# FFN inputs turned on TensorE instead of by DMA, h written as z(1+y), and block 0's butterflies on TensorE, in a long-convolution plus SwiGLU kernel

## The chip, the cores and the metric

The kernel runs on one core of a Trainium2 chip. The metric is the device time of one execution in microseconds (us). The kernel before takes 307.82 us, the median of three runs.

In this text PE is TensorE, DVE is VectorE, ACT is ScalarE, POOL is GpSimd and SP is SyncE, which here only issues DMAs.

## What is computed

A sequence of 2048 rows of 640 features goes through two stages. With `LN` a layer normalization without gain or bias:

```python
def _A_ref(q, k, v, shift_k, ssm_k, ssm_D):     # q is LN(A_q)
    k_shift = sum(k_pad[:, t:t+S, :] * shift_k[:, 3-t] for t in range(4))
    kv = k_shift * v
    y = irfft(rfft(kv_pad) * rfft(ssm_k_pad))[:, :S]    # causal convolution over the sequence
    return q * (y + kv * ssm_D)
h  = A_q + _A_ref(LN(A_q), A_k, A_v, ...)
h2 = h + (silu(LN(h) @ w_gate) * (LN(h) @ w_up)) @ w_down
```

S is 2048, the FFN has 1728 hidden features, and inputs and output are bf16.

## The kernel before

**Tiling.** The sequence is cut into four blocks of 512 rows. The convolution is a product of block transforms: each block of kv is transformed by cosine and sine matmuls (`x_transform`, L725), each block of the filter likewise (`g_transform`, L670), the products are summed over pairs of blocks on DVE (L939, L975, L979, L999, L1000), and `back` brings block i into the time domain (L810). A transformed block is two "lanes" of 128 x 3 x 1280 numbers; the third part is the sum of the first two and serves the three-multiplication complex product. Lanes that are needed later go to DRAM and come back.

**Forward transform.** For each block it makes sums over the even and over the odd rows separately (eight PSUM tiles of 128 x 640 with four matmuls each, L725). ACT or DVE evacuates them. Then four DVE operations, the butterflies, form sum (L735) and difference (L738), and two more form the third part (L742).

**From convolution to h.** `ln_stats` takes mean and mean square of each row group of x with two ACT passes (L750, L752), a few tiny DVE operations and one power on POOL (L764). `back` writes z = x - mean (L796). y comes out of PSUM scaled by 1/sigma (L397). DVE multiplies z by y (L816) and adds x (L817); this is h. `ln_stats` then runs on h, for the first pair of row groups (r = 0) and for the second (r = 1).

**FFN input.** Two DVE passes for each r write hn = LN(h) (L824). Each of a block's four row groups of 128 x 640 is then turned by one DMA transpose on SP's queue (`tr_dma`, L595) into `hlnT`, the right-hand side of the FFN's first matmuls.

**FFN.** 27 groups of five matmuls of 128 x 512 (L873) give gate and up features. ACT writes silu of gate (L877) and a copy of up (L878), DVE multiplies them into `tT` (L880). Then 112 matmuls with `w_down` and 8 with the identity, which add h (L894, L897), fill four PSUM tiles; ACT evacuates them into `o` (L902), which POOL's queue sends out. FFN weights stream through three buffers by SP's queue.

**What sets the order.** The whole program is written as a list of operations with durations and priorities. A planner (`Plan.schedule`) simulates the engines and picks on each engine the next operation by the earliest start and then by priority. The table `DELTA` moves priorities of single groups. The result is one fixed order on each engine's queue, and every queue is worked off in that order: PE, DVE, ACT, POOL and SP each wait at the head of their queue. There are four PSUM tiles (`ps`) of two banks each.

**The options.** `OPT` chooses variants. `EITHER_G`, `OADD_PE` and `LN_EITHER` are the same before and after; the fourth of before, `DIAG`, is empty. Functions for the shift by diagonal matrices exist in both kernels and are not used in either.

Of the kernel before, what the change touches and what calls it, by code (L numbers as in the profile page):

```python
# [30 lines left out]
    "C0 ACT back": 6020,  # L31
    "C0 ACT evac": -5111,
    "C0 ACT ln_stats": 2613,
    "C0 DVE shift": -1855,
    "C0 SP gb_t": 2038,
    "C0 SP gst": 3,
    "C0 SP v": 391,
    "C1 DVE ln_stats": -1020,
    "C1 DVE prod": 2265,
    "C1 SP wd": 2582,  # L40
    "C2 ACT ln_stats": -4955,
    "C2 DVE ln_stats": 250,
    "C2 DVE x_transform": 2472,
    "C3 ACT ln_stats": 302,
    "C3 DVE back": -1149,
    "C3 DVE last": -2417,
    "C3 DVE ln_stats": -580,
    "C3 DVE psum": 3611,
    "C3 DVE shift": 3075,
    "F1 DVE ffn": 100,  # L50
    "F2 ACT down": 2947,
    "G0 DVE g_fold": -14579,
    "G0 PE g_transform": -1010,
    "G1 DVE g_sum": -713,
    "G1 SP gst": 2010,
    "G2 ACT g_sum": 15743,
    "G2 DVE g_fold": 1994,
    "G3 ACT evac": 2112,
    "G3 DVE g_sum": -1154,
    "G3 PE g_transform": -5601,  # L60
# [245 lines left out]
def kernel(  # L306
# [735 lines left out]
```

## Time and profile before

| what | value |
|---|---|
| median of 3 runs | 307.82 us (307.66 to 310.0) |
| the profiled execution's own time | 308.64 us |
| its span, first to last instruction | 306.7 us |
| PE busy | 255.5 us, 83% |
| DVE busy | 223.8 us, 73% |
| ACT busy | 195.4 us, 64% |
| mean granted TensorE clock | 0.951 of full speed |

The own time of the profiled execution is 1.94 us more than its span: something lies before the first and after the last instruction. Busy time of PE is modelled for pipelined matmuls and can't be read as useful work; the rate of a long run of matmuls without a wait can.

### The profile page before, as it was taken

How to read it: one execution, taken by the hardware profiler on the slowest of the kernel's cores; microseconds unless marked ns; L12 is line 12 of the kernel's file. 1: busy time of each engine (PE TensorE's matmuls, PEld its weight loads, DVE VectorE, ACT ScalarE, POOL GpSimd, SP SyncE). 2: the span in 40 equal slices, each digit the busy share in tenths (PEclk: the TensorE clock that was granted, in tenths of full speed). 3: DMA queues.
4: the chain of work that ended last, by engine and by line, in shares of the span. 5: the costliest groups of instructions: out<-in, count | busy, mean ns of one | idle time of the engine just before them, and what ended most of it. 6: DMA issues, size and time to landing. Idle time of an engine off the chain costs nothing.

```text
span 306.7 us, 4036 instructions
## 1 busy us (share of the span) xinstructions
PE 255.5 (83%) x1440; PEld 143.3 (47%) x1440; DVE 223.8 (73%) x302; ACT 195.4 (64%) x363; POOL 31.7 (10%) x38
## 2 busy tenths in 40 slices
PE   0388366196999999978998799699999999999993
PEld 0166233063444567733445467345445774444671
DVE  1799999998499999787999989859899630212100
ACT  1168998885999586559818982048974873454310
POOL 2000103210102005200100003100012021000000
PEclk9999788578899999999999999989999999999998
DMA  7969659999799896996535997993646033660011
GB/s 179 347 207 254 190 221 312 290 315 225 239 340 259 282 340 205 306 340 171 130 70 137 352 244 237 266 372 119 153 107 172 2 87 94 164 150 0 2 43 43
DMA packets 72088, 61.09 MB, mean 199 GB/s; under 512 B 31171, under 2 KB 67204, under 8 KB 71558
## 3 DMA queue, kind: packets, MB, share of 16 engines
q1 hardware_dynamic: 70126, 50.32, 60.0%
q0 software_dynamic: 1792, 10.49, 9.2%
q8 instruction: 11, 0.18, 0.2%
q14 instruction: 9, 0.07, 0.1%
q10 hardware_dynamic: 150, 0.04, 0.1%
HBM read 45.76 MB, written 10.49 MB: 183 GB/s over the span
## 4 chain that ended last, share of the span: by engine, by line
PE 25%; DVE 21%; ACT 20%; issue 19%; DMA 9%; SPq 2%; POOL 2%; ACTq 0%; POOLq 0%; DVEq 0%
PE ps L873 14%; ACT junk L750 5%; PE ps L897 5%; DMA hlnT<-s 4%; ACT junk L752 4%; DVE wk L703 4%; ACT uc L878 3%; ACT sg L877 3%; PE ps L810 2%; DVE wk L708 2%; DMA hlnT<-in_A_shift_k_dram 2%; SPq L595 2%; ACT lane L395 2%; PE ps L670 2%; DMA wk<-in_A_q_dram 2%
## 5 line engine op out<-in xcount | busy, mean ns | idle before, releaser
L873 PE MATMUL ps<-hlnT,wgu 128*128 128x512 bf16 x540 | 122.3, 386 | 11.1 <-DMA hlnT<-s 8.1
L873 PEld LDWEIGHTS <-wgu 128*128 128x128 bf16 x540 | 53.4, 99 | 78.6 <-issue 16.4
L877 ACT ACTIVATE sg<-ps 128x512 bf16<-128x512 f32 (+1 forms) x56 | 33.7, 602 | 46.5 <-PE ps L873 32.0
L897 PE MATMUL ps<-wdA,tT 128*128 128x320 bf16 x384 | 55.4, 299 | 0.0
L880 DVE TENSOR_TENSOR tT<-sg,uc 128x512 bf16<-128x512 bf16 (+1 forms) x56 | 23.4, 420 | 42.1 <-ACT uc L878 42.0
L897 PEld LDWEIGHTS <-tT 128*128 128x128 bf16 x448 | 43.8, 98 | 17.0
L670 PE MATMUL ps<-wgu,gb_t 128*128 128x320 bf16 x128 | 25.4, 353 | 12.9 <-DMA wgu<-wk 12.5
L764 POOL TENSOR_TENSOR mv<-mv,mhalf 128x2 f32<-128x2 f32 (+1 forms) x12 | 19.0, 1587 | 144.2 <-DVE mv L762 126.1
L878 ACT CAST uc<-ps 128x512 bf16<-128x512 f32 (+1 forms) x56 | 32.8, 585 | 0.4 <-PE ps L873 0.3
L902 ACT CAST o<-ps 128x640 bf16<-128x640 f32 x16 | 11.0, 687 | 31.9 <-PE ps L897 31.9
L975 DVE TENSOR_TENSOR lane<-lane,lane 128x3840 bf16<-128x3840 bf16 x12 | 25.8, 2151 | 2.7 <-DMA lane<-hd 2.2
L810 PE MATMUL ps<-eo,ci_t 128*128 128x320 bf16 x128 | 20.0, 307 | 7.7 <-DVE eo L785 2.6
L395 ACT CAST lane<-ps 128x640 bf16<-128x640 f32 x39 | 24.7, 728 | 1.8 <-PE ps L670 1.7
L670 PEld LDWEIGHTS <-gb_t 128*128 128x128 bf16 x128 | 14.2, 113 | 22.8 <-issue 11.9
L703 DVE TENSOR_TENSOR wk<-krun,w 128x2560 bf16<-128x2560 bf16 (+1 forms) x20 | 24.0, 1217 | 0.2
L810 PEld LDWEIGHTS <-ci_t 128*128 128x128 bf16 x128 | 12.7, 100 | 14.8 <-issue 9.5
L725 PE MATMUL ps<-wk,cs_t 128*128 128x320 bf16 x128 | 18.7, 298 | 0.9 <-DVE wk L709 0.7
L708 DVE TENSOR_TENSOR wk<-wk,wk 128x2560 bf16<-128x2560 bf16 (+1 forms) x15 | 18.1, 1217 | 0.0
L725 PEld LDWEIGHTS <-cs_t 128*128 128x128 bf16 x128 | 12.3, 97 | 7.0 <-issue 1.3
L750 ACT ACTIVATE junk<-wk 128x640 bf16<-128x640 bf16 x16 | 11.9, 743 | 3.8 <-DMA wk<-in_A_q_dram 3.6
L397 ACT ACTIVATE s<-ps,mv 128x640 bf16<-128x640 f32 x16 | 12.3, 796 | 3.0 <-PE ps L810 2.8
L750 ACT ACTIVATE junk<-h 128x640 bf16<-128x640 bf16 x16 | 11.9, 742 | 2.3 <-DVE h L817 2.0
(76 smaller groups left out, 272.1 us busy)
## 6 DMA issues: line engine op xcount, KB each, us to landing
wgu<-in_B_w_gate_dram SPq DMA_DIRECT2D x24, 320.0 KB, 3.9
wgu<-in_B_w_up_dram SPq DMA_DIRECT2D x24, 320.0 KB, 4.1
lane<-xd SPq DMA_DIRECT2D x6, 960.0 KB, 6.1
lane<-hd SPq DMA_DIRECT2D x6, 960.0 KB, 6.7
xd<-lane POOLq DMA_DIRECT2D x4, 960.0 KB, 7.0
hd<-lane POOLq DMA_DIRECT2D x4, 960.0 KB, 5.3
krun<-in_A_k_dram SPq DMA_DIRECT2D x3, 1120.0 KB, 5.4
wk<-in_A_v_dram SPq DMA_DIRECT2D x4, 640.0 KB, 6.7
```

What stands on the lines that cost most here:

```text
L395: nc.scalar.copy(dst(), src())
L670: nc.tensor.matmul(ps.t[:, h, 0:NH], wt, mv, start=(k == 0), stop=(k == len(ks) - 1))
L703: nc.vector.tensor_mul(dst.t[:, sl, :], ks, w4.t[:, j:j + 1, :].broadcast_to([P, n, D]))
L708: dve(c, lambda sl=sl: nc.vector.tensor_add(kv.t[:, sl, :], kv.t[:, sl, :], tm.t[:, sl, :]), [(kv, m), (tm, m)], [(kv, m)])
L725: nc.tensor.matmul(ps.t[:, h, 0:NH], cs_t.t[:, s, n, c * P:(c + 1) * P], kv.t[:, s, h * NH:(h + 1) * NH], start=(a == 0), stop=(a == 1))
L750: act(0.73, lambda s=s: nc.scalar.activation(junk.t[:], x.t[:, s, :], ACT.Identity, scale=-1.0 / D, accum_out=mv.t[:, s:s + 1]), [(x, 1 << ...
L810: nc.tensor.matmul(ps.t[:, hh, 0:NH], ci_t.t[:, c, 1 - n, s, :], x.t[:, 2 * pos[n] + c, hh * NH:(hh + 1) * NH], start=(k == 0), stop=(k == 3))
L873: nc.tensor.matmul(ps.t[:, k, :], wg.t[:, kt, off:off + P], hT.t[:, kt, :], start=(kt == 0), stop=(kt == NDC - 1))
L877: act(c_act(MBLK) + 0.02, lambda ps=ps, sg=sg, np_=np_: nc.scalar.activation(sg.t[0:np_, :], ps.t[0:np_, 0, :], ACT.Silu), [(ps, 1)], [sg])
L878: act(c_act(MBLK), lambda ps=ps, uc=uc, np_=np_, lo=up_lo, k=len(offs) - 1: nc.scalar.copy(uc.t[0:np_, :], ps.t[lo:lo + np_, k, :]), [(ps, ...
L897: nc.tensor.matmul(ps.t[:, hh, 0:NH], tv()[:, c, m * P:(m + 1) * P], wdc(c)[:, hh * NH:(hh + 1) * NH], start=(c == 0 and not oadd), stop=( ...
L975: dve(c_tt(6 * D), lambda xl=xl, hl=hl: nc.vector.tensor_mul(xl.t[:], xl.t[:], hl.t[:]), [xl(), hl()], [xl()], name="prod")
```

## The change

1. `HT_PE = (0, 1, 2)`: in blocks 0 to 2 hn is turned by ten PE transposes for each r into one PSUM tile, which ACT or DVE copies into `hlnT`. Block 3 keeps its four DMA transposes.
2. `HN_ACT = (1, 2, 3)`: hn of blocks 1 to 3 is written by ACT (scale and bias per row), with one tiny DVE product for the bias.
3. h is kept without its mean: y is evacuated as 1 + y/sigma (a bias of one), h' = z(1 + y), and the second DVE operation of h, the addition of x, is gone. `LN(h)` doesn't depend on a constant per row. The mean comes back as the bias with which ACT evacuates the FFN's result; a tiny DVE operation keeps it per block.
4. `BF_PE = (0,)`: block 0's butterflies are done by PE: each of the eight output tiles takes eight matmuls instead of four, half of the difference tiles with negated constants `csm_t`, which one ACT pass makes.
5. `XEARLY`: block 0's x is loaded, and its statistics are ordered, before block 0's transform.
6. `ST_ALT = (0,)`: block 0's mean squares of h may go to DVE; in the order that results all of them are on ACT.
7. `DELTA` is another table (some 60 entries), an offset `slack` lets SP and PE prefer a later operation of higher priority, and the planner's costs of a DMA transpose are changed (280 KB and 0.3 us instead of 160 KB and 0.6 us). So the order is another one everywhere.

Core of the diff:

```diff
-OPT = (True, (0, 1, 2, 3), (0,), ())
+OPT = (True, (0, 1, 2, 3), (0,), (), (0, 1, 2), (1, 2, 3), True, (0,), (0,), 0)
-    EITHER_G, OADD_PE, LN_EITHER, DIAG = OPT
+    EITHER_G, OADD_PE, LN_EITHER, TSH, HT_PE, HN_ACT, XEARLY, BF_PE, ST_ALT, NHALF = OPT
-    pl.slack = {}
+    pl.slack = {e: 0.05 * DELTA.get(f"slack {e}", 0) for e in Plan.LAT}
...
+        if i in BF_PE:
+            for e in range(2):
+                for n in range(2):
+                    for c in range(2):
+                        ps = B("ps")
+                        for r in range(2):
+                            def mm(ps=ps, r=r, n=n, c=c, e=e):
+                                for a in range(2):
+                                    s = 2 * a + r
+                                    w = (csm_t.t[:, a] if r and e else cs_t.t[:, s])[:, n, c * P:(c + 1) * P]
+                                    for h in range(2):
+                                        nc.tensor.matmul(ps.t[:, h, 0:NH], w, kv.t[:, s, h * NH:(h + 1) * NH], ...)
...
-                evac(D, lambda y=y, a=a: v2(y.t[:, a, :]), lambda ps=ps: r3(ps.t), [ps, (mvx, 16 << s)], [(y, 1 << a)], i == 0,
-                     lambda s=s: mvx.t[:, NS + s:NS + s + 1])
+                pl.op("ACT", c_act(D), lambda ...: nc.scalar.activation(v2(y.t[:, a, :]), r3(ps.t), ACT.Identity, bias=one.t[:], scale=mvx.t[:, NS + s:NS + s + 1]), ...)
             dve(c_tt(2 * D), lambda sl=sl, y=y: nc.vector.tensor_mul(h.t[:, sl, :], h.t[:, sl, :], y.t[:]), ...)
-            dve(c_tt(2 * D), lambda sl=sl: nc.vector.tensor_add(h.t[:, sl, :], h.t[:, sl, :], xt.t[:, sl, :]), ...)
...
+                if i in HN_ACT:
+                    act(c_act(D), lambda ...: nc.scalar.activation(hn.t[:, a, :], h.t[:, s, :], ACT.Identity, bias=mv.t[:, 3 * NS + s:3 * NS + s + 1], scale=mv.t[:, NS + s:NS + s + 1]), ...)
+                if i not in HT_PE:
+                    tr_dma(lambda s=s: hT.t[:, :, s * P:(s + 1) * P], lambda hn=hn, a=a: hn.t[:, a, :], [(hn, 1 << a)], [(hT, 1 << s)], name="hT")
+            if i in HT_PE:
+                def tr(ps=ps, hn=hn):
+                    for a in range(2):
+                        for c in range(NDC):
+                            nc.tensor.transpose(pt[:, a, c * P:(c + 1) * P], hn.t[:, a, c * P:(c + 1) * P], ident.t[:])
+                pl.op("ACT", c_act(2 * D), lambda dst=dst, src=turned: nc.scalar.copy(dst(), src()), [ps], [(hT, 5 << r)],
+                      alt=[("DVE", 0.8, lambda dst=dst, src=turned: nc.vector.tensor_copy(dst(), src()))], name="hT")
...
-                    act(c_act(D), lambda ps=ps, m=m: nc.scalar.copy(v2(o.t[:, m, :]), r3(ps.t)), [ps], [(o, 1 << m)], name="down")
+                    act(c_act(D), lambda ps=ps, m=m: nc.scalar.activation(v2(o.t[:, m, :]), r3(ps.t), ACT.Identity, bias=mean[f"x{i}"].t[:, m:m + 1]), ...)
```

DVE around block 0's FFN input, before: `s` are the buffers of hn, `h_86` is h, `wk` and `krun` belong to block 1's shift, `lane` to products of transforms.

```order
L761 TENSOR_TENSOR mv_100<-mv_100 128x2
L762 SCALAR_TENSOR_TENSOR mv_100<-mv_100 128x2
L824 TENSOR_SCALAR s_1_82<-h_86,mv_99 128x640 x2
L708 TENSOR_TENSOR wk_75<-wk_75,wk_74 128x2560
L824 TENSOR_SCALAR s_0_81<-h_86,mv_100 128x640 x2
L709 TENSOR_TENSOR wk_75<-wk_75,wk_76 128x2560
L678 TENSOR_TENSOR lane_71<-lane_71 128x1280
L975 TENSOR_TENSOR lane_67<-lane_67,lane_70 128x3840
```

The same place on DVE after (L938 is hn, L1134 the product, L833 and L836 block 1's butterflies, L959 a copy of turned hn).

```order
L789 TENSOR_TENSOR wk_77<-wk_77,wk_73 128x2560
L758 TENSOR_TENSOR lane_72<-lane_72 128x1280
L863 TENSOR_TENSOR mv_100<-mv_100 128x2
L864 SCALAR_TENSOR_TENSOR mv_100<-mv_100 128x2
L1134 TENSOR_TENSOR lane_67<-lane_67,lane_69 128x3840
L863 TENSOR_TENSOR mv_99<-mv_99 128x2
L864 SCALAR_TENSOR_TENSOR mv_99<-mv_99 128x2
L938 TENSOR_SCALAR s_1_82<-h_86,mv_100 128x640 x2
L1134 TENSOR_TENSOR lane_68<-lane_68,lane_70 128x3840
L938 TENSOR_SCALAR s_0_81<-h_86,mv_99 128x640 x2
L833 TENSOR_TENSOR lane_70<-wk_73,lane_69 128x1280 x2
L959 COPY hlnT_94<-ps_64 128x2x5x128
```

Block 1's shift (its last step is L709, L789 after) and both products stood partly behind hn and now stand in front of its second half, and a copy out of PSUM follows two butterflies.

ACT where block 1's FFN begins, before: four evacuations of block 2's transform into a lane, the first silu (`sg`), block 2's eight row statistics (`junk`), the first `uc`.

```order
L395 CAST lane_69<-ps_63 128x640
L395 CAST lane_69<-ps_64 128x640
L395 CAST lane_69<-ps_66 128x640
L395 CAST lane_69<-ps_65 128x640
L877 ACTIVATE sg_96<-ps_63 128x512
L750 ACTIVATE junk,mv_99<-wk_75 128x640
L752 ACTIVATE junk,mv_99<-wk_75 128x640
...
L752 ACTIVATE junk,mv_99<-wk_75 128x640
L878 CAST uc_97<-ps_63 128x512
L877 ACTIVATE sg_95<-ps_65 128x512
```

The same place on ACT after (L852 and L854 are the statistics, L901 is z of block 2, L1027 and L1028 `sg` and `uc`).

```order
L449 CAST lane_72<-ps_66 128x640
L852 ACTIVATE junk,mv_99<-wk_76 128x640
L854 ACTIVATE junk,mv_99<-wk_76 128x640
L901 ACTIVATE h_86<-wk_76,mv_99 128x640
L852 ACTIVATE junk,mv_99<-wk_76 128x640
L854 ACTIVATE junk,mv_99<-wk_76 128x640
L901 ACTIVATE h_86<-wk_76,mv_99 128x640
L852 ACTIVATE junk,mv_99<-wk_76 128x640
L1027 ACTIVATE sg_96<-ps_66 128x512
L901 ACTIVATE h_86<-wk_76,mv_99 128x640
L1028 CAST uc_97<-ps_66 128x512
L854 ACTIVATE junk,mv_99<-wk_76 128x640
```

Five statistics and two z stand before the first silu now, and no row of eight stands between it and its `uc`.

## Rows read from the trace of the kernel before

**Rows 1.** Busy us by stage (windows), cut at each FFN's begin; clock, DMA share, GB/s last.

```profile
0.00:74.40 74.40, 40.02 (x229) 24.41 (x230) 64.89 (x91) 52.70 (x88) 9.29 (x14) 0.86 0.90 251
74.40:133.40 59.00, 56.76 (x320) 31.55 (x321) 50.53 (x67) 43.97 (x83) 9.89 (x10) 0.97 0.93 286
133.40:197.00 63.60, 55.72 (x320) 31.04 (x321) 58.57 (x78) 40.92 (x80) 5.58 (x6) 1.00 0.75 205
197.00:255.80 58.80, 57.40 (x320) 31.59 (x321) 43.84 (x55) 39.93 (x80) 5.32 (x5) 0.97 0.53 154
255.80:306.70 50.90, 45.55 (x255) 24.75 (x253) 5.95 (x14) 17.89 (x32) 1.62 (x3) 0.97 0.25 68
```

**Rows 2.** PE's waits: engine, line, waited for, us in total, times, longest.

```profile
PE ps L873 <- DMA hlnT<-s: 8.1, 4, 2.8
PE ps L873 <- ACT uc L878: 2.8, 3, 1.5
PE ps L810 <- ACT uc L878: 1.5, 2, 1.0
```

**Rows 3.** PE's timeline: start, us, line, tiles, count, idle before and its releaser.

```profile
15.69 2.32 PE L606 MATMUL ps<-ident,wk 128*128 128x128 bf16 x20 [4.98 <-DVE wk L636]
...
74.38 27.16 PE L873 MATMUL ps<-hlnT,wgu 128*128 128x512 bf16 x115 [2.56 <-DMA hlnT<-s]
...
133.38 8.79 PE L873 MATMUL ps<-hlnT,wgu 128*128 128x512 bf16 x40 [1.99 <-DMA hlnT<-s]
...
197.00 8.32 PE L873 MATMUL ps<-hlnT,wgu 128*128 128x512 bf16 x30 [2.83 <-DMA hlnT<-s]
...
255.59 29.30 PE L873 MATMUL ps<-hlnT,wgu 128*128 128x512 bf16 x135 [0.70 <-DMA hlnT<-s]
...
300.72 0.71 PE L897 MATMUL ps<-wdB,tT 128*128 128x320 bf16 x4
```

**Rows 4.** The chain that ended last: start, us, what.

```profile
89.50 10.97 PE ps L873 x50
...
136.23 0.83 ACT junk L750 x2
...
142.31 0.83 ACT junk L752 x2
...
251.08 3.82 PE ps L897 x28
```

**Rows 5.** DVE's timeline: block 0's shift begins, and its second hn.

```profile
10.92 2.29 DVE L703 TENSOR_TENSOR wk<-krun,w 128x1280 bf16<-128x1280 bf16 x3
...
65.03 0.80 DVE L824 TENSOR_SCALAR s<-h,mv 128x640 bf16<-128x640 bf16 x2
```

**Rows 6.** DMA issues: tiles, engine, count, KB each, us from issue to landing.

```profile
wgu<-in_B_w_gate_dram SPq DMA_DIRECT2D x24, 320.0 KB, 3.9
...
wgu<-in_B_w_gate_dram SPq DMA_DIRECT2D x4, 160.0 KB, 3.5
...
hlnT<-s SPq DMA_TRANSPOSE x16, 5.9
```

**Rows 7.** Groups of instructions by shape: count, busy us, mean ns, idle before.

```profile
L975 DVE TENSOR_TENSOR lane<-lane,lane 128x3840 bf16<-128x3840 bf16 x12 | 25.8, 2151 | 2.7 <-DMA lane<-hd 2.2 <-DMA lane<-xd 0.6
...
L395 ACT CAST lane<-ps 128x640 bf16<-128x640 f32 x39 | 24.7, 728 | 1.8 <-PE ps L670 1.7
...
L708 DVE TENSOR_TENSOR wk<-wk,wk 128x2560 bf16<-128x2560 bf16 x9 | 13.3, 1482 | 0.0
L796 ACT ACTIVATE h<-wk,mv 128x640 bf16<-128x640 bf16 x16 | 13.1, 839 | 0.0
...
L824 DVE TENSOR_SCALAR s<-h,mv 128x640 bf16<-128x640 bf16 x16 | 6.4, 442 | 2.3 <-POOL mv L764 2.3
...
L608 ACT COPY wgu<-ps 128x1280 bf16<-128x1280 bf16 x2 | 2.4, 1229 | 5.5 <-PE ps L606 5.5
...
L401 DVE CAST w<-ps 128x640 bf16<-128x640 f32 x2 | 1.6, 825 | 7.3 <-PE ps L486 7.3
```

More of the change, by code (lines that the diff above doesn't have):

```diff
@@ L30 @@
 DELTA = {
[L31 to L60, printed above, removed]
+    "C0 ACT hT": -13889,
+    "C0 ACT lnx": 3360,
+    "C0 ACT y": -17094,
+    "C0 DVE comb": -156622,
+    "C0 DVE eo0": -152679,
+    "C0 DVE eo1": -150639,
+    "C0 DVE gate": 113,
@@ new lines @@
+    "C1 DVE comb": -14865,
+    "C1 DVE eo0": -9321,
+    "C1 DVE eo1": -4075,
+    "C1 DVE gate": -151352,
+    "C1 DVE hmul0": -8741,
+    "C1 DVE join0": -9631,
+    "C1 DVE last": -14864,
+    "C1 DVE nm": 2413,
+    "C1 DVE prod": -14867,
+    "C1 DVE shift": -151669,
+    "C1 DVE tinyx": -9341,
+    "C1 DVE xsum0": -14797,
+    "C1 PE x1": -1900,
+    "C1 SP k": -170567,
+    "C2 ACT lnh0": 4622,
+    "C2 DVE bfly0": -16074,
+    "C2 DVE bfly1": -14040,
+    "C2 DVE comb": -14120,
+    "C2 DVE eo1": -16349,
@@ new lines @@
+    "C2 DVE gate": 2108,
+    "C2 DVE hmul0": -11849,
+    "C2 DVE last": -16084,
+    "C2 DVE shift": 3319,
+    "C2 DVE tinyh0": 4877,
+    "C2 DVE tinyh1": 7425,
+    "C2 DVE tinyx": -14164,
+    "C2 DVE xsum0": -13856,
+    "C3 ACT hn": -19906,
+    "C3 ACT lnh1": -170653,
+    "C3 ACT lnx": 2456,
+    "C3 ACT y": -170623,
+    "C3 DVE bfly0": -1517,
+    "C3 DVE bfly1": -2547,
+    "C3 DVE eo0": -2099,
+    "C3 DVE eo1": -1811,
+    "C3 DVE hmul0": -171486,
+    "C3 DVE join0": -1801,
+    "C3 DVE join1": -171785,
@@ new lines @@
+    "C3 DVE last": -1085,
+    "C3 DVE prod": -3567,
+    "F0 ACT down": 8593,
+    "F0 DVE ffn": -8669,
+    "F0 PE down": 11323,
+    "F1 ACT down": 5826,
+    "F1 DVE ffn": -17020,
+    "F1 PE down": 3773,
+    "F1 SP w": -156619,
+    "G1 DVE g_sum": -150749,
+    "G1 SP gst": -361,
+    "G2 ACT gev": -199,
+    "G2 ACT half": 3008,
+    "G2 DVE g_fold": 69,
+    "G2 DVE g_sum": -15905,
+    "G3 ACT gev": -18178,
+    "G3 DVE g_fold": -2869,
+    "G3 PE g_transform": -1899,
+    "slack PE": 1,
@@ L451 @@
     s0c = [Fixed(f"s0c{p}", (P, NDC, 1)) for p in range(NB - 1)]
-    klead = Fixed("klead", (P, NDC, NS, 1))
     mhalf = Fixed("mhalf", (P, NS), FP32)
     junk = Fixed("junk", (P, D))
+    junkd = Fixed("junkd", (P, D))
+    one = Fixed("one", (P, 1), FP32)
+    mean = {f"x{i}": Fixed(f"mean{i}", (P, NS), FP32) for i in range(NB)}
     H0 = [Lane(Fixed(f"h0_{e}", (P, 3, 2, D))) for e in range(2)]
@@ new lines, in q, with mm @@
+            def q(x, half=half):
+                return x.rearrange("p (a t) -> p a t", a=2) if half else x
+            hm, tm = ((5 << lo, 1 << c) if lo == 0 else (5 << lo, 1 << (16 + c))) if half else (15, 1 << c | 1 << (16 + c))
+            for k, off in enumerate(offs):
+                def mm(ps=ps, k=k, off=off, wg=wg, rr=rr, q=q, w=w):
+                    for kt in range(NDC):
+                        nc.tensor.matmul(q(ps.t[:, k, 0:w]), wg.t[:, kt, off:off + P], rr(hT.t[:, kt, :]), start=(kt == 0), stop=(kt == NDC - 1))
+                with pl.at(FFN[i] + (20 * lo if half else 0)):
+                    pe(NDC * (0.112 if half else c_mm(512)), mm, [(wg, bits if c == 13 else 1 << k), (hT, hm)], [(ps, 1 << k)], alloc=[tT], name=f"half{lo}" if half else "up")
```

309 lines of the change are left out of this document (195 added, 114 removed).

## The prediction

> **What bounds the kernel now.** I read the busy time by stage first, cut where each block's FFN begins [rows 1]. Up to 74.4 us PE is busy for 40.0 us and DVE for 64.9: the opening belongs to DVE, with ACT close behind (52.7). From there on PE is the bound: 56.8 of 59.0, 55.7 of 63.6, 57.4 of 58.8 us, and nearly all of the last stage. Busy PE isn't useful PE, so I take its rate from long runs in the chain: 50 FFN matmuls in 10.97 us, 0.219 each, and 28 of the 320-wide ones in 3.82 us, 0.136 each [rows 4]. From 74.38 to 301.43 us (300.72 + 0.71) [rows 3] PE does 540 of the former, 118.5 us, and 672 of the latter (480 for the results, 96 and 64 for two transforms, 32 for the last filter block), 91.7 us: 210.2 us of work in 227.05, so 16.9 us are lost there. By stage, each between the starts in [rows 3]: 54.7 us of work in 59.0, in 63.6 and in 58.6, so 4.3, 8.9 and 3.9 lost, and nothing in the last. What PE waits for is then in the waits [rows 2]: 8.1 us for turned FFN inputs (2.56, 1.99, 2.83, 0.70 in [rows 3]; the first lies before 74.38) and 4.3 for ACT's `uc`. After the third of these entries 30 matmuls take 8.32 us, 1.7 more than at 0.219 [rows 3].
>
> **The change part by part.** Time is start of FFN 0, plus PE's work, plus what it loses, plus the end.
>
> *Start of FFN 0.* Before, the second hn ends at 65.83 [rows 5] and FFN 0 begins at 74.38 [rows 3]: 8.55 us for four transposes, which land 5.9 us after their issue [rows 6]. When does hn end now? From the first tap at 10.92 [rows 5] DVE has hardly a gap, so I count its queue up to the second hn. It loses four butterflies and two additions of x, but block 1's shift and both first products are now ahead of hn. In all: 46 operations of 1280 numbers become 42, 4 x 0.76 = -3.0 (three in 2.29, [rows 5]); one more of 2560, +1.5, one more of 3840, +2.15, one evacuation fewer, -0.8, two z at 0.44, +0.9 [rows 7]; two scalings of a filter lane, which ACT did, at some 0.5 each, +1.0 (an estimate from the 0.44 for half the numbers). Sum +1.7: hn ends at 67.5 by DVE alone. ACT gets nine evacuations more ahead of its last statistics of h (9 x 0.73 = +6.6), and loses two z (-1.7) and one scaling (-1.2, the 1.23 row) [rows 7]; the negated constants fall into the time when it waits for the first turned filter (5.5 us idle at L608 [rows 7]). That is +3.7 us, part of which its waits absorb. I take 68 (67.5 to 69.5). Then ten transposes, 1.2 (20 in 2.32, [rows 3]), and a copy out of PSUM: ACT's row for this shape is 1.23, DVE's for half of it 0.83 [rows 7], so 0.8 to 1.7; I take 1.2. For the hand-offs I take 0.8 (0 to 1.5, no row prices them). FFN 0 starts at 71.2 (69.5 to 74.4), 3.2 earlier.
>
> *The 32 extra matmuls of block 0* (4.4 us) lie in a stage where PE has 34 idle us [rows 1]; without that cover they cost 4.4. Each output tile now needs both halves of kv, so its evacuations begin later; that is in ACT's bound above.
>
> *PE's work from then on.* Blocks 1 and 2 add 40 transposes, 40 x 0.116 = 4.6 us [rows 3]: 214.8.
>
> *What PE loses.* FFN 0's stage: the wait of 1.99 before FFN 1 goes, since its transposes stand among the result matmuls with 112 still needing other things; 4.3 becomes 2.5. FFN 1's stage: the wait of 2.83 goes. In its opening ACT does block 2's eight statistics in one row, 136.2 to 143.1 [rows 4], between the first silu and its `uc`; the new order has five ahead, of which the transform's earlier place (before the last four result groups) gives them 4 us, and three spread out. DVE, 58.6 busy of 63.6 [rows 1], loses two additions and four hn per block, 2 x 0.76 + 4 x 0.44 = 3.3. Of the 4.3 waited for `uc` I let 3.5 go: 8.9 becomes 2. FFN 2's stage: no wait at its entry, so no slow run after it, 1.7; 3.9 becomes 1. The 0.70 of block 3 stays. Sum 5.5 instead of 16.9. Lower bound 2.5 (a slow start of 1.7 after FFN 0's entry, as after the third one, and the 0.7), upper 12.1 (only the two waits go).
>
> *Work moved to ACT.* Twelve hn at 0.84 and, of the six copies at 1.23, four on ACT: 15 us more in stages where it is busy for 44.0 of 59.0 and 40.9 of 63.6 [rows 1]. I cost it nothing since it falls under PE's result matmuls (120 x 0.136 = 16 us per block); without that cover it is the rival below. Behind a copy that waits for PE stand, on ACT in block 0, the last scaling, the table load and the first silu, and on DVE block 1's second butterflies, which nobody needs before their evacuation to DRAM.
>
> *SP.* Twelve transposes of 1.3 us leave its queue; block 1's x, which stood behind four of them, comes earlier. Block 0's x and the second filter block go earlier too, ahead of v or the third filter block; DVE needs v only some 15 us into its taps, so I put nothing. The 1 + y, the mean as a bias and the mean's copy ride on passes that exist: under 0.2 us each, off the path but for the last result tile.
>
> *Sum.* 71.2 + 214.8 + 5.5 + 5.3 (306.7 - 301.43) = 296.8 us of span. Own time of the profiled execution is 1.94 more, 298.7 against 308.64; the median of the runs lies 0.82 under that own time, so 297.9; I say 298.
>
> The DMA transposes are the point where the Trainium skill speaks against the change: "Advanced Engine Details and Errata", section X-Bar Transpose (TRN2), says that transposing transfers are as fast as plain ones. Here the row has 5.9 us for 160 KB (128 x 640 bf16) against 3.5 for plain loads of 160 KB and 3.9 for 320 KB [rows 6], so the trace doesn't agree, as they are queued here. By the page the turned inputs would cost no more than 3.5, 2.4 less at each of three entries, and the sum would be about 7 us higher, near 305; by the row it stands.
>
> **The rivals.**
> *FFN 0 doesn't start earlier.* For it: DVE and ACT both get more ahead of hn. Against it: 8.55 us of transposing become about 3. Start 74.4, the rest as above, 300.0 of span: 301.1.
> *The DMA engines are the limit.* They are at 0.90 and 0.93 in the first two stages [rows 1]; then transposes only waited for bandwidth, weights and lanes are late in their place, and PE's losses shrink by just the two waits. 74.4 + 214.8 + 12.1 + 5.3 = 306.6, by the same offsets 307.7: no change. Against it: stages 3 and 4 run at 0.75 and 0.53 and still wait. The skill's rule above leans to this rival; the landing times lean away.
> *ACT ends the waits at the entries (slower).* Place: FFN 1's and FFN 2's begin. hn, the copies, the result evacuations and the next block's eight transform evacuations are one queue. If the second copy ends up behind the eight, an entry waits for 2 x 0.84 + 1.23 + 8 x 0.73 = 8.7 us. Twice is 17.4 more: 315. It decides from about 6.5 us at each entry, where 298 becomes 311. For it: ACT is 15 us fuller. Against it: in the new order the second copy of block 1 stands before the eight.
>
> **How the numbers follow.** Forecast 0.62; FFN 0 not earlier 0.20; DMA limit 0.10; ACT at the entries 0.08. A measurement of this kernel can tell about 1% from no change, (3.1 us), so the first two are faster, 0.82; the third is the same, 0.10; the fourth slower, 0.08. Own range: start 69.5 and losses of 2.5 give 293.2, start 72 and losses of 9 give 302. The range reaches down to 291 for unpriced hand-offs and up to 306, past the second rival and short of the third.
>
> **What would show it.** Right: PE's first FFN matmul at 69.5 to 72; waits for `hlnT` only at block 3's entry, under 1.5 us in total after FFN 0; stage 2 at 58 to 59, stage 3 near 60, stage 4 at 54 to 56; 40 transposes on PE after that start. Wrong: FFN 0 at 74 or later; PE waiting for L958 or L959 by more than 2 us an entry; a `wgu` load as the releaser of FFN matmuls; stage 3 still over 63.

## The result, and the profile after

The kernel after takes 298.24 us (median of 4 runs, 297.55 to 298.45) against 308.26 for the kernel before: ratio 0.9662, 95% interval 0.9618 to 0.9706. The prediction was 298.0. The profiled execution took 297.55 us with a span of 295.8; before it was 308.64 with 306.7.

The windows of the kernel after, cut where each FFN begins; columns as in [rows 1].

```profile
0.00:69.00 69.00, 42.17 (x281) 27.92 (x282) 59.92 (x90) 52.47 (x89) 10.35 (x15) 0.95 0.98 291
69.00:126.80 57.80, 56.32 (x336) 32.20 (x340) 55.27 (x70) 50.10 (x93) 6.29 (x7) 1.00 0.80 267
126.80:188.30 61.50, 58.96 (x354) 33.85 (x356) 55.75 (x74) 51.54 (x99) 5.97 (x6) 1.00 0.69 210
188.30:244.00 55.70, 52.70 (x302) 29.52 (x302) 37.29 (x48) 37.04 (x67) 4.63 (x7) 1.00 0.48 130
244.00:295.80 51.80, 45.60 (x252) 24.88 (x255) 5.95 (x14) 18.49 (x33) 1.62 (x4) 0.97 0.24 67
```

By the begins of the FFNs (in [rows 3] and in the timeline below) the first stage is 5.4 us shorter, the next three 1.2, 2.1 and 2.8; the last is 0.7 longer, all of it behind the last matmul. DVE is now busy for 55.3 of 57.8 us in FFN 0's stage, and ACT, with 50.1, 51.5 and 37.0, is 6 to 11 us fuller than before in two of the three.

The granted clock of TensorE, the third column from the end, was 0.97, 1.00 and 0.97 in the three FFN stages [rows 1] and is 1.00 in all three now. Two stretches of 2 us in the kernel before, behind the entries of FFN 0 and FFN 2, and one of the kernel after, behind that of FFN 0:

```profile
76.00:78.00 2.00, 2.00 (x6) 0.64 (x5) 0.00 (x0) 1.46 (x3) 0.00 (x0) 0.50 1.18 308
199.00:201.00 2.00, 2.00 (x6) 0.76 (x5) 0.16 (x1) 0.41 (x1) 0.00 (x0) 0.50 1.08 451
```

```profile
71.00:73.00 2.00, 2.00 (x11) 0.91 (x10) 2.00 (x4) 1.65 (x4) 0.00 (x0) 1.00 1.01 415
```

Behind its waits of 2.56 and 2.83 us PE ran for some time at 0.50, the lower of the clock's two levels (1.2 of 2.4 GHz), with 6 matmuls in 2 us instead of 11. At 0.219 each [rows 4] the 115 matmuls behind the first wait would take 25.2 us and took 27.16, the 30 behind the other 6.6 and took 8.32 [rows 3]. These 2.0 and 1.7 us the kernel after doesn't lose. Why an entry gets the lower clock stays open: in evac_first, below, FFN 0 begins behind a wait of 1.56 us as it does here, and runs at 0.67 and then 0.50.

Then the timeline of the kernel after around each FFN's begin: start, us, engine and line, tiles, count, and the idle time before with its releaser.

```profile
10.33 2.29 DVE L783 TENSOR_TENSOR wk<-krun,w 128x1280 bf16<-128x1280 bf16 x3
...
65.56 0.80 DVE L938 TENSOR_SCALAR s<-h,mv 128x640 bf16<-128x640 bf16 x2
65.66 0.72 PE L950 MATMUL ps<-ident,s 128*128 128x128 bf16 x10
66.71 0.72 PE L950 MATMUL ps<-ident,s 128*128 128x128 bf16 x10 [0.33 <-ACT lane L449]
67.09 1.30 ACT L958 COPY hlnT<-ps 128x1280 bf16<-128x1280 bf16 x1
68.03 0.82 DVE L959 COPY hlnT<-ps 128x1280 bf16<-128x1280 bf16 x1
68.99 6.20 PE L1023 MATMUL ps<-hlnT,wgu 128*128 128x512 bf16 x27 [1.56 <-DVE hlnT L959]
...
126.81 13.43 PE L1023 MATMUL ps<-hlnT,wgu 128*128 128x512 bf16 x59
...
188.29 2.32 PE L1023 MATMUL ps<-hlnT,wgu 128*128 128x512 bf16 x9
191.81 4.48 PE L1023 MATMUL ps<-hlnT,wgu 128*128 128x512 bf16 x20 [1.19 <-ACT o L1052]
...
244.04 4.26 PE L1023 MATMUL ps<-hlnT,wgu 128*128 128x512 bf16 x18 [0.69 <-issue]
...
289.17 0.71 PE L1047 MATMUL ps<-wdB,tT 128*128 128x320 bf16 x4
```

The reader sees the new way from hn to the FFN: the second hn ends at 66.36, ten transposes take 0.72 us, DVE's copy ends at 68.85, and FFN 0 starts at 68.99 instead of 74.38 [rows 3]. Ahead of it stands the first tap of the shift, at 10.33 here and at 10.92 before [rows 5]. From first tap to FFN 0 it is 58.66 us against 63.46. Below this difference is used for openings, since the first tap came between 10.33 and 11.42 in kernels whose work up to there is the same.

PE's waits of the kernel after, against [rows 2]:

```profile
PE ps L1023 <- DVE hlnT L959: 1.6, 1, 1.6
PE ps L1023 <- ACT o L1052: 1.2, 1, 1.2
PE ps L1044 <- ACT hlnT L958: 0.9, 1, 0.9
PE ps L1044 <- ACT wk L449: 0.8, 1, 0.8
PE ps L1044 <- ACT o L1052: 0.8, 1, 0.8
PE ps L1023 <- ACT uc L1028: 0.4, 1, 0.4
```

No line names a DMA of `hlnT` as what PE's matmuls waited for: 7.4 of the 8.1 us are gone. The 0.7 at block 3's entry is still there, put down to `issue` in the timeline; the last of block 3's DMA transposes, which land 2.6 to 3.1 us after their issue, is issued at 241.2 us. The 2.8 us for `uc` became 0.4. What is new are waits for ACT: for an evacuated result tile (`o`) and for the copy `hlnT`.

Last, the groups by shape that the change added or altered.

```profile
L919 ACT ACTIVATE s<-ps,one,mv 128x640 bf16<-128x640 f32 x16 | 14.1, 907 | 1.0 <-PE ps L915 0.8
L1052 ACT ACTIVATE o<-ps,mean 128x640 bf16<-128x640 f32 x16 | 12.5, 789 | 15.2 <-PE ps L1047 15.1
L935 ACT ACTIVATE s<-h,mv 128x640 bf16<-128x640 bf16 x12 | 10.5, 923 | 0.1
L958 ACT COPY hlnT<-ps 128x1280 bf16<-128x1280 bf16 x4 | 5.0, 1239 | 1.3 <-PE ps L950 1.3
L950 PE MATMUL ps<-ident,s 128*128 128x128 bf16 x60 | 4.5, 219 | 0.5 <-ACT lane L449 0.3
L959 DVE COPY hlnT<-ps 128x1280 bf16<-128x1280 bf16 x2 | 1.6, 822 | 0.8 <-PE ps L950 0.8
```

### The profile page after: what moved, and what is told of

Same layout as the page of the kernel before. It is cut to its first block, busy times and chain, and to the rows that moved or that the text cites. A ratio compares the mean times of both kernels' runs of the same rounds, so it can differ in the third digit from the quotient of the medians.

```text
span 295.8 us, 4183 instructions
## 1 busy us (share of the span) xinstructions
PE 255.8 (86%) x1519; PEld 148.4 (50%) x1532; DVE 214.2 (72%) x294; ACT 209.7 (71%) x377; POOL 28.9 (10%) x38
## 2 busy tenths in 40 slices
DMA packets 64025, 59.15 MB, mean 200 GB/s; under 512 B 23106, under 2 KB 59139, under 8 KB 63493
## 4 chain that ended last, share of the span: by engine, by line
PE 25%; ACT 24%; DVE 21%; issue 20%; DMA 6%; SPq 1%; POOL 1%; ACTq 0%; POOLq 0%; DVEq 0%
PE ps L1023 19%; ACT junk L852 5%; ACT junk L854 4%; DVE wk L783 4%; PE ps L1047 3%; ACT s L919 2%; DVE eo L890 2%; DVE lane L1134 2%; DVE wk L788 2%; ACT uc L1028 2%; DMA hlnT<-in_A_shift_k_dram 2%; ACT sg L1027 2%; PE ps L823 2%; DMA wgu<-in_B_w_up_dram 2%; DMA wgu<-wk 2%
## 5 line engine op out<-in xcount | busy, mean ns | idle before, releaser
L1023 PE MATMUL ps<-hlnT,wgu 128*128 128x512 bf16 x527 | 118.1, 379 | 4.7 <-DVE hlnT L959 1.6
L1027 ACT ACTIVATE sg<-ps 128x512 bf16<-128x512 f32 (+1 forms) x56 | 33.5, 598 | 44.2 <-PE ps L1023 29.7
L1028 ACT CAST uc<-ps 128x512 bf16<-128x512 f32 (+1 forms) x56 | 32.7, 584 | 0.3 <-PE ps L1023 0.2
L1134 DVE TENSOR_TENSOR lane<-lane,lane 128x3840 bf16<-128x3840 bf16 x12 | 25.8, 2153 | 2.2 <-DMA lane<-hd 2.1
L449 ACT CAST lane<-ps 128x640 bf16<-128x640 f32 x42 | 26.1, 739 | 0.8 <-PE ps L750 0.8
L868 POOL TENSOR_TENSOR mv<-mv,mhalf 128x2 f32<-128x2 f32 (+1 forms) x12 | 16.4, 1365 | 103.1 <-DVE mv L864 67.6
L1052 ACT ACTIVATE o<-ps,mean 128x640 bf16<-128x640 f32 x16 | 12.5, 789 | 15.2 <-PE ps L1047 15.1
L750 PE MATMUL ps<-wgu,gb_t 128*128 128x320 bf16 x128 | 20.5, 304 | 1.9 <-ACT lane L449 1.3
L823 PE MATMUL ps<-wk,cs_t 128*128 128x320 bf16 x96 | 16.3, 330 | 5.7 <-DVE wk L789 5.5
L750 PEld LDWEIGHTS <-gb_t 128*128 128x128 bf16 x128 | 12.7, 99 | 8.2 <-issue 2.8
L823 PEld LDWEIGHTS <-cs_t 128*128 128x128 bf16 x96 | 10.1, 107 | 11.7 <-DVE wk L789 6.1
L919 ACT ACTIVATE s<-ps,one,mv 128x640 bf16<-128x640 f32 x16 | 14.1, 907 | 1.0 <-PE ps L915 0.8
L852 ACT ACTIVATE junk<-h 128x640 bf16<-128x640 bf16 x16 | 11.8, 740 | 3.1 <-DVE h L923 2.5
L1138 DVE TENSOR_TENSOR lane<-lane,lane 128x3840 bf16<-128x3840 bf16 x6 | 12.9, 2156 | 0.1
```

The lines of the kernel that those rows point to most:

```text
L750: nc.tensor.matmul(ps.t[:, h, 0:NH], wt, mv, start=(k == 0), stop=(k == len(ks) - 1))
L823: nc.tensor.matmul(ps.t[:, h, 0:NH], cs_t.t[:, s, n, c * P:(c + 1) * P], kv.t[:, s, h * NH:(h + 1) * NH], start=(a == 0), stop=(a == 1))
L852: act(0.73, lambda s=s: nc.scalar.activation(junk.t[:], x.t[:, s, :], ACT.Identity, scale=-1.0 / D, accum_out=mv.t[:, s:s + 1]), [(x, 1 << ...
L1023: nc.tensor.matmul(q(ps.t[:, k, 0:w]), wg.t[:, kt, off:off + P], rr(hT.t[:, kt, :]), start=(kt == 0), stop=(kt == NDC - 1))
L1027: act(c_act(w) + 0.02, lambda ps=ps, sg=sg, np_=np_, w=w: nc.scalar.activation(sg.t[0:np_, 0:w], ps.t[0:np_, 0, 0:w], ACT.Silu), [(ps, 1)] ...
L1028: act(c_act(w), lambda ps=ps, uc=uc, np_=np_, lo=up_lo, k=len(offs) - 1, w=w: nc.scalar.copy(uc.t[0:np_, 0:w], ps.t[lo:lo + np_, k, 0:w]), ...
```

## The experiments

"Start" is FFN 0's begin less the first tap. Ratios are to the kernel before, run on the same chip; it took 308.0 to 309.0 us there (medians), so a difference between two rows of the table is good to about 1 us.

| kernel | median us | ratio, 95% interval | start us |
|---|---|---|---|
| before | 308.26 | 1 | 63.46 |
| after | 298.24 | 0.9662, 0.9618 to 0.9706 | 58.66 |
| turn0_dma | 311.94 | 1.0131, 1.0069 to 1.0192 | 68.96 |
| turn0_first | 305.03 | 0.9878, 0.9821 to 0.9934 | 60.38 |
| turn12_dma | 304.32 | 0.9892, 0.9821 to 0.9964 | 58.48 |
| plain_copies | 305.75 | 0.9917, 0.9879 to 0.9955 | 61.91 |
| pass_more | 305.52 | 0.9883, 0.9840 to 0.9925 | 60.21 |
| bfly_more | 302.37 | 0.9786, 0.9745 to 0.9828 | 61.83 |
| turn_alone | 325.11 | 1.0558, 1.0485 to 1.0631 | 62.29 |
| no_table_after | 332.65 | 1.0771, 1.0649 to 1.0894 | |
| no_table_before | 336.78 | 1.0914, 1.0810 to 1.1018 | |
| hn_dve | 296.50 | 0.9604, 0.9546 to 0.9662 | 58.76 |
| hn_dve23 | 295.10 | 0.9549, 0.9510 to 0.9589 | 59.07 |
| evac_first | 295.59 | 0.9549, 0.9501 to 0.9598 | 58.51 |

**Block 0 by DMA again (turn0_dma).**

```diff
+BY_DMA = (0,)
 def tr(ps=ps, hn=hn, i=i):
+    if i in BY_DMA:
+        return
...
+def by_dma(hn=hn, r=r, hT=hT):
+    for a in range(2):
+        s = 2 * a + r
+        nc.sync.dma_start_transpose(out=hT.t[:, :, s * P:(s + 1) * P], in_=hn.t[:, a, :])
...
-pl.op("ACT", c_act(2 * D), lambda dst=dst, src=turned: nc.scalar.copy(dst(), src()), ...)
+def cp(copy, dst=dst, src=turned, by_dma=by_dma, i=i):
+    by_dma() if i in BY_DMA else copy(dst(), src())
+pl.op("ACT", c_act(2 * D), lambda cp=cp: cp(nc.scalar.copy), ...)
```

> The kernel after with block 0's FFN input turned by four DMA transposes again, issued by SP where the copies out of PSUM stood; every other instruction and its order is kept. Theory 1 (the DMA transposes' landing time set the start of FFN 0): hn ends at 66.4 us as before the edit, the last transpose lands some 6 to 8 us later, FFN 0 starts at 73 to 75 instead of 69.0, and the whole is 4 to 6 us longer, 302 to 304 us. Rival (the earlier start comes from the new order and the lighter DVE, the transposes were hidden): FFN 0 at 69 to 70, 298 to 299 us.

Its SP queue and PE's entry in the timeline:

```profile
56.16 0.34 SPq L472 DMA_DIRECT2D krun<-in_A_k_dram  x1
56.55 0.88 SPq L472 DMA_DIRECT2D wk<-in_A_q_dram  x1
57.53 0.64 SPq L472 DMA_DIRECT2D wk<-in_A_v_dram  x1
64.67 10.62 SPq L964 DMA_TRANSPOSE hlnT<-s  x4
...
80.37 0.59 PE L1032 MATMUL ps<-hlnT,wgu 128*128 128x512 bf16 x1 [12.98 <-DMA hlnT<-s]
```

Theory 1 holds, and its price was set far too low: the start is 10.3 us later, the whole 13.7. The transposes wait behind k, x and v of later blocks (1120, 640 and 640 KB), which the new order issues at 56 to 58 us; before, x and v were issued at 71.7 and 73.7, behind the transposes (k in front of them there too, at 62.3). The transposes' landing took 9.6 to 13.0 us here. Of the 3.4 us beyond the start, 2.7 are lost right behind PE's wait of 13 us: up to its next wait for `uc` FFN 0 takes 15.94 us instead of 13.24, with a granted clock of 0.50 to 0.61 from 80.3 to 86.3 us.

**The same with those loads behind the transposes (turn0_first).**

```diff
+LATE = ("C1 SP x", "C2 SP k", "C2 SP v")
...
+    late = [o for o in order[:last] if o.key in LATE]
+    order = [o for o in order[:last + 1] if o not in late] + late + order[last + 1:]
```

> As the run with block 0's FFN input turned by DMA, but the loads of block 2's k and v and of block 1's x, which stood in front of the transposes on SP's queue and filled the DMA engines, are issued behind them. If the landing time is made by what is under way in front of the transposes: they land 3 to 6 us after issue instead of 9.6 to 13, FFN 0 starts at 72 to 75 us instead of 80.4, and the whole takes 300 to 305 us. Rival (a DMA transpose is slow by itself): FFN 0 not before 78, 308 us or more.

PE's entry, and ACT's wait from 60 to 135 us:

```profile
71.11 8.32 PE L1033 MATMUL ps<-hlnT,wgu 128*128 128x512 bf16 x30 [3.97 <-DMA hlnT<-s]
```

```profile
ACT junk L854 <- DMA wk<-in_A_q_dram: 4.1, 1, 4.1
```

Now the transposes land 2.6 us after their issue (median; 11.3 in turn0_dma), and the start is only 1.7 us later than with PE, so a DMA transpose without these loads ahead of it costs little at this entry. But the time is 6.8 us up: the loads come too late, ACT stands 4.1 us before block 1's x with silu and `uc` queued behind it, PE then waits 2.9 us for `uc`, and FFN 0's stage is 63.1 us instead of 57.8. Behind both of PE's waits the granted clock is low as well, 0.50 from 73.1 to 75.1 us and 0.53 from 82.4 to 86.0; the 30 matmuls above take 8.32 us, 1.7 more than at 0.219. So either the turned input or the loads are late; turning on PE takes the input out of that queue. By these two runs, that is what turning on PE saves at FFN 0's entry in this order; the lighter DVE queue, below, is another part of the earlier start.

**Blocks 1 and 2 by DMA again (turn12_dma).** The same edit with `BY_DMA = (1, 2)`.

> The kernel after with the FFN inputs of blocks 1 and 2 turned by DMA transposes again, in an order that is otherwise kept; block 0 stays on PE. Theory 1: the waits for turned inputs at the entries of FFN 1 and FFN 2 come back with 2 to 3 us each, less 1.4 us for each block's transposes and PE's part, so 3 to 5 us longer, 301 to 303 us. Rival (the new order already has hn early enough): no wait for hlnT at the two entries, 297 to 298.5 us.

Its timeline, ACT and PE:

```profile
119.12 1.73 ACT L936 ACTIVATE s<-h,mv 128x640 bf16<-128x640 bf16 x2 [8.21 <-DMA hlnT<-s]
...
121.72 6.18 PE L824 MATMUL ps<-wk,cs_t 128*128 128x320 bf16 x32 [4.37 <-ACT o L1061]
...
193.72 6.63 PE L1032 MATMUL ps<-hlnT,wgu 128*128 128x512 bf16 x29 [1.96 <-DMA hlnT<-s]
```

6.1 us slower, so the waits were real, but the larger one is another than expected: the transposes hold the buffer `s` of the first hn, ACT waits 8.2 us before it can write the second, the result evacuations stand behind that, and PE waits 4.4 us for a PSUM tile. The wait for turned inputs itself came back at FFN 2 alone, 2.0 us. The planner gave `s` away early because PE frees it early, so a part of this price belongs to the order.

**Plain copies in place of the transposes (plain_copies).**

```diff
-tr_dma(lambda s=s: hT.t[:, :, s * P:(s + 1) * P], lambda hn=hn, a=a: hn.t[:, a, :], ...)
+pl.op("SP", 1.25, lambda ...: nc.sync.dma_start(out=hT.t[:, :, s * P:(s + 1) * P], in_=hn.t[:, a, :].rearrange("p (k t) -> p k t", k=NDC)), ..., nbytes=160 * KB, fix=0.6, ...)
```

> The kernel before with each of the 16 DMA transposes of the FFN inputs replaced by a plain DMA of the same 160 KB between the same tiles, at the same place of SP's queue; so the FFN inputs aren't turned and the output is another. If the transposing itself is slow: the median landing falls from 5.9 to about 3.5 us, PE's waits for hlnT from 8.1 us to under 3, and the time by 5 to 8 us, to 300 to 303. If the transposes only wait for DMA engines and queue that are busy with other loads: landing stays within 1 us of 5.9, the waits stay, and the time is 307 to 309.

The SP entries for `hlnT`, duration min/median/max in ns, of the kernel before and of this one:

```profile
L595 SPq DMA_TRANSPOSE hlnT<-s x16: 1211/1304/3112, 63.6 to 252.7; - x16
```

```profile
L827 SPq DMA_DIRECT2D hlnT<-s x16: 593/624/3349, 63.2 to 251.0; - x16
DMA to landing us min/median/max: 2.8/6.2/7.8
```

The median landing is 6.2 us, not shorter than 5.9 [rows 6]: for the landing the second theory stands. A transpose does hold SP longer, 1.30 us against 0.62; PE's waits for `hlnT` fall to 5.1 us, the start comes 1.55 us earlier, and the time falls by 0.8%, a third to a half of what the first theory wanted and more than the second allowed. That this rest is SP's queue wasn't tried apart.

**DVE passes put back (pass_more, bfly_more).**

```diff
 nc.vector.tensor_mul(h.t[:, sl, :], h.t[:, sl, :], y.t[:])
+nc.vector.tensor_tensor(h.t[:, sl, :], h.t[:, sl, :], h.t[:, sl, :], op=ALU.max)
```

> The kernel after with one more DVE pass over h (a maximum of h with itself, 128x1280) behind each of the eight products z(1+y), at the place and of the size of the addition of x that the change removed; order kept. Each costs 0.75 us of DVE, 6.0 in all. Theory 1 (DVE sets the opening and FFN 1's stage): block 0's two passes put FFN 0 off by 1.5 us, block 2's cost up to 1.5, the others are covered: 300 to 302 us. Rival (DVE has room everywhere, ACT and PE pace the rest): within 1 us of 298.2.

```diff
+for n in range(2):
+    nc.vector.tensor_tensor(X[e].t[:, n], X[e].t[:, n], X[e].t[:, n], op=ALU.max)
 nc.vector.tensor_add(X[e].t[:, 2], X[e].t[:, 0], X[e].t[:, 1])
```

> The kernel after with four more DVE passes (maximum of a lane part with itself, 128x1280) in block 0's transform, as many and as large as the butterflies that went to PE; order kept. 4 x 0.75 = 3.0 us of DVE before FFN 0. Theory 1 (the opening is bound by DVE): FFN 0 starts 2 to 3 us later, 300 to 301.5 us. Rival (the nine us in which DVE is idle before FFN 0 take them in): FFN 0 at most 1 us later, within 1 us of 298.2.

First tap and FFN 0's begin in the timelines of pass_more and of bfly_more:

```profile
11.42 2.29 DVE L783 TENSOR_TENSOR wk<-krun,w 128x1280 bf16<-128x1280 bf16 x3
...
71.63 14.92 PE L1026 MATMUL ps<-hlnT,wgu 128*128 128x512 bf16 x60 [1.84 <-DVE hlnT L962]
```

```profile
11.24 2.29 DVE L783 TENSOR_TENSOR wk<-krun,w 128x1280 bf16<-128x1280 bf16 x3
...
73.07 13.24 PE L1027 MATMUL ps<-hlnT,wgu 128*128 128x512 bf16 x60 [1.56 <-DVE hlnT L963]
```

Two passes put the start off by 1.55 us, four by 3.17: 0.75 to 0.8 for each pass of 0.75. Up to FFN 0 every DVE pass counts in full, so the opening is bound by DVE, though DVE is idle for 9 of its 69 us. In pass_more 7.3 us come out of 6.0 us of passes. By the starts of the FFNs (71.63, 132.75, 194.71, 252.15) the stages are 3.3, 0.5 and 1.7 us longer. But 1.7 of the 3.3 are the clock's: the first 60 matmuls of FFN 0 take 14.92 us, with 0.55 granted from 71.6 to 73.6, against 13.24 at 1.00 in bfly_more and in the kernel after. Without that the stages are some 1.6, 0.5 and 1.7 us longer, so the passes cost something in FFN 0's and FFN 2's stages and little in FFN 1's, where theory 1 had put it. My upper bound of 4 us was too low.

**One part alone, and both kernels without a table.** turn_alone puts the code of the PE transposes into the kernel before, with `HT_PE = (0, 1, 2)` and its old table; in the other two the table is emptied:

```diff
-DELTA = {...}
+DELTA = {}
```

> The kernel before with the first part of the change alone: blocks 0 to 2 turned on PE; table, h, butterflies and loads as before, the order planned anew with the old table. Theory 1 (the turning on PE is what saves): FFN 0 starts 4 to 6 us before 74.4, no waits for hlnT at FFN 1 and FFN 2, 298 to 303 us. Rival (the saving is the new order and the lighter DVE): 305 to 310 us.

> The kernel after with an empty table: no group's priority is moved and no offset for SP and PE, so the planner orders it by its own rules. Theory 1 (the parts themselves save): it is 5 to 12 us faster than the kernel before with an empty table, and both lie above their own tabled versions, at 305 to 330 us. Rival (the gain is made by the new table): the two without a table are within 3 us of each other, or the order is reversed.

> The kernel before with an empty table, the other half of the comparison. Theory 1: 5 to 12 us slower than the kernel after with an empty table. Rival: within 3 us of it, or faster.

PE's waits in turn_alone, and in the kernels after and before without a table:

```profile
PE ps L811 <- ACT uc L897: 8.8, 3, 6.9
PE ps L726 <- ACT wk L396: 5.4, 1, 5.4
```

```profile
PE ps L938 <- DMA hlnT<-s: 15.8, 1, 15.8
```

```profile
PE ps L842 <- DMA hlnT<-s: 30.6, 2, 17.0
```

turn_alone falls outside both theories, 17 us slower than before, and its FFN 0 starts only 1.2 us earlier from the first tap. Its PE has no DMA wait for `hlnT` at FFN 1 and FFN 2, yet the three stages take 65.9, 66.7 and 66.4 us: PE waits for ACT's evacuations, 5.4 us and up to 6.9 in one wait. That the old table doesn't fit the new operations is the likely reason, but it was not shown apart; the run says what the part gives with that order and nothing of what it could give. Without a table the kernel after is 4.1 us faster than the kernel before. All four of its runs (331.06 to 335.49) lie below all four of the other's (336.03 to 340.39), so it is very likely faster; by how much is less sure, and 4.1 lies between the two theories. The waits agree: 30.6 us of waiting for `hlnT` before, at the entries of FFN 0 and FFN 3; after, 15.8 at FFN 3 alone, and that one is still turned by DMA. But FFN 0 begins no earlier there, 64.78 us from the first tap against 63.82, so little of the 17.0 us of waiting that went is saved. The tables are worth 28.5 us before and 34.4 after. So some 4 of the 10 us are there without a table, and the rest only with an order made for the new parts. `XEARLY`, `ST_ALT` and the planner's other costs weren't tried apart.

**hn on DVE again (hn_dve, hn_dve23, evac_first).**

```diff
-nc.scalar.activation(hn.t[:, a, :], h.t[:, s, :], ACT.Identity, bias=..., scale=...)
+nc.vector.tensor_scalar(hn.t[:, a, :], h.t[:, s, :], mv.t[:, s:s + 1], mv.t[:, NS + s:NS + s + 1], op0=ALU.add, op1=ALU.mult)
```

> The kernel after with hn of blocks 1 to 3 written by DVE again (12 x 0.44 = 5.3 us more there, 12 x 0.92 = 11 us less on ACT), at the same places of the order. Theory 1 (these passes lie beside PE's result matmuls on either engine): within 1 us of 298.2. Rival 1 (ACT ends waits at the entries): 1 to 3 us faster. Rival 2 (DVE's relief was what shortened FFN 1's stage): 1 to 4 us slower.

hn_dve23 does this for blocks 2 and 3 alone (`if i > 1`), and evac_first moves one ACT operation in addition:

```diff
+order.remove(ev), order.insert(order.index(zs[0]), ev)
```

> The kernel after with hn of blocks 2 and 3 written by DVE, that of block 1 by ACT; order kept. In the run with all three on DVE, FFN 0's stage was 1.3 us longer than in the kernel after (59.15 against 57.82), FFN 1's 1.6 and FFN 2's 2.0 us shorter (59.89 against 61.48, 53.72 against 55.75). Theory 1 (each block's hn belongs on the engine that has room in that stage, and the effects add): 57.8, 59.9 and 53.7 us, a span of 292 and 293 to 295.5 us by time, ratio to before 0.950 to 0.957. Rival (the difference between the runs is noise): 297 to 299 us, ratio 0.962 to 0.968.

> As the run before it, and the third evacuation of FFN 1's result stands on ACT in front of block 3's four z instead of behind them and one statistic. Theory 1 (PE's wait of 1.19 us at FFN 2's entry for that tile is made by these five operations in front of it): the wait goes, FFN 2's stage is 1 to 1.3 us shorter than in the run before it, 292 to 294.5 us. Rival (PE then waits for the next thing, silu's tiles or the last evacuation): within 0.5 us of the run before it.

Windows of hn_dve23 for FFN 0 to FFN 2, then PE's timeline at FFN 2's entry in evac_first:

```profile
70.10:127.90 57.80, 56.48 (x340) 32.18 (x341) 55.18 (x70) 50.10 (x94) 6.29 (x7) 1.00 0.79 266
127.90:187.80 59.90, 58.89 (x358) 33.75 (x356) 55.97 (x77) 49.03 (x95) 5.99 (x6) 1.00 0.67 200
187.80:242.80 55.00, 52.97 (x305) 29.48 (x302) 39.84 (x54) 32.84 (x62) 4.19 (x6) 1.00 0.54 147
```

```profile
188.26 4.48 PE L1028 MATMUL ps<-hlnT,wgu 128*128 128x512 bf16 x20
192.99 2.32 PE L1028 MATMUL ps<-hlnT,wgu 128*128 128x512 bf16 x10 [0.25 <-ACT o L1057]
```

Rival 1 of hn_dve is nearest, though its interval overlaps that of the kernel after. In blocks 2 and 3 hn is better on DVE, in block 1 on ACT (FFN 0's stage 59.15 us in hn_dve, 57.8 in hn_dve23). In blocks 2 and 3 it may be that ACT has no room, or that the pass itself is shorter on DVE, some 440 ns [rows 7] against 923; the runs don't separate these. hn_dve23 at 295.10 us beats both kernels, its interval lies below that of the kernel after, by 3.1 us of the medians; 1.6 of them are in FFN 1's stage, 0.7 in FFN 2's in this profile, where 2.0 had been expected. In evac_first the wait of 0.77 us at FFN 2's entry (1.19 in the kernel after) is down to 0.25, and FFN 2's stage is 1.0 us shorter, as theory 1 has it. But the time is the same as that of hn_dve23 within the interval, so the gain isn't shown. In the profile of evac_first FFN 0's stage, where nothing was changed, is 1.7 us longer: its first 60 matmuls take 14.92 us instead of 13.24, at a granted clock of 0.67 and 0.50 in its first 4 us. That alone can hide 1 us.

## Why the prediction was right, step by step

**Start of FFN 0.** Predicted 3.2 us earlier, measured 5.4, of which 0.6 is the earlier first tap. hn: DVE's count gave +1.7, I took 68 for ACT's sake; from the first tap it is +1.1, and ACT's part didn't show; that DVE sets it is what bfly_more and pass_more show. Way from hn to FFN: 2.63 us against the 3.2 of the sum; the transposes take 0.72 where [rows 3] gave 1.2, copy and hand-offs 1.9 where I had 2.0.

**PE's work.** 40 transposes by 0.072 are 2.9 us, not 4.6. The row that I scaled, 20 in 2.32, has weight loads of 145 ns behind a wait of 5 us; the 60 of the kernel after have 97. The granted clock is 1.00 in both, so why they differ stays open. The 32 extra matmuls of block 0 show no cost, as costed: in front of FFN 0 PE waits for DVE. No run takes them apart.

**What PE loses.** By the rates of [rows 4] the three stages hold 56.2, 58.3 and 52.5 us of work (one half of block 3's transform, 16 matmuls, and so 2.2 us, moved from FFN 2's stage into FFN 1's) and take 57.82, 61.48 and 55.75. So 1.7, 3.1 and 3.2 are lost where 2.5, 2 and 1 were predicted: 8.0 instead of 5.5. FFN 0's stage is better because the slow start behind its entry, 2.0 us at the lower clock, is gone; the prediction had let the slow start go at FFN 2 alone, and it had put it down to the wait and not to the clock. The other two are worse, and the waits name most of the cause: 3.7 of the 6.3 us are waits for `o`, `hlnT` and `wk`, all evacuated by ACT, and 0.7 is block 3's entry; the rest is not named by a wait above.

**Work moved to ACT** is the step that failed. I cost it nothing, as covered by PE's result matmuls; hn_dve23 says that the eight hn of blocks 2 and 3 cost about 3 us there (3.1 by the medians, 2.3 by the stages of the two profiles). The third rival had the right engine and place, at a seventh of its price: 1.19 us of waiting at FFN 2's entry instead of 8.7, and not in front of the copy but of a result tile.

**The sum.** Start −2.2, PE's work and losses together +0.6 (−1.7 for the transposes, +2.5 for the losses, −0.2 for the last stage, whose 46.0 us by the rates took 45.8), the end +0.6 (the last transfer takes 0.55 longer): 295.8 us of span for 296.8. Errors of opposite sign make it look better than its parts. The last step was luck too: the span is 1.0 us under the forecast, and the median comes back to 298.24 because it lies 0.69 us above the profiled execution's own time, where 0.82 below had been taken. Of the signs, the start (68.99) and stage 2 (57.8) came just under their ranges, and stage 3 (61.5) above its "near 60".

**The other rivals.** "FFN 0 doesn't start earlier" is refuted. "The DMA engines are the limit" is refuted as a forecast, but right on the cause: the transposes did wait for the DMA engines. The median 5.9 [rows 6] mixed two cases, as the issues of the kernel before show when its windows are taken apart, block 0 first (60 to 80 us, where the DMA engines move 260 GB/s) and then block 3 (245 to 257 us, 83 GB/s):

```profile
hlnT<-s SPq DMA_TRANSPOSE x4, 6.7
...
hlnT<-s SPq DMA_TRANSPOSE x4, 3.1
```

So my reading against the Trainium skill's section X-Bar Transpose (TRN2) in "Advanced Engine Details and Errata" was wrong: in landing time transposes and plain copies agree here, 5.9 and 6.2 us, as the Trainium skill says. The sum of 305 by the Trainium skill doesn't follow either, since what the change takes away is the queue and not the transposing.

## What to carry to other kernels

A median time to landing says nothing on the operation until it is split by how full the DMA engines are, and moving a small urgent transfer onto an idle engine pays twice: it no longer waits, and the large loads may go ahead of it. Work moved onto another engine "under cover" needs a price for each stage; here four of twelve passes were best on ACT and the other eight cost about 3 us there. A wait at an entry can cost more than its length: behind waits of 1.6 to 13 us some profiles ran at the lower clock and lost some 1.7 to 2.7 us more, others didn't, so stages are compared at equal granted clock. Parts that were fitted together by an order lose more when taken out alone (13.7, 6.1, 7.3 and 4.1 us for a gain of 10), so such numbers don't add.

## What the runs showed that had not been expected

The first load, 5 KB of filter taps, lands at 7.70 to 8.84 us and shifts the whole opening with it, so profiles of one opening differ by up to 1.1 us; differences from the first tap agree within 0.6 us. Transposes on PE in runs of ten take 0.072 us each. An evacuation by ACT with a bias takes 0.1 us more than without (907 ns against 796, and 789 against 687), and DVE copies 128x1280 bf16 out of PSUM in 0.82 us where ACT takes 1.24.
